# Convolution block with GRN: which blocks keep their activations on chip, where stored blocks are loaded, and the layout of the last twelve blocks

## The chip, the cores and the metric

The kernel runs on one core of one Trainium2 chip. The metric is the device time of one execution in microseconds, the median of several runs. The engines are named as in the profile: PE (matrix products), PEld (its weight loads), DVE (vector), ACT (activation functions), POOL (general purpose, here elementwise sums and the issue of some DMAs) and SP (issue of DMAs).

## The reference

The input x is an image of 512 x 512 pixels with 96 channels in bfloat16. What has to be computed, cut to its core (C = 96, E = 384 hidden channels):

```python
out = depthwise 3x3 convolution of x with dw          # zero padding
h = (out - mean_c(out)) / sqrt(var_c(out) + 1e-5)     # per pixel, over channels
h = gelu(h @ w1)                                      # [512*512, 384], tanh form
gx = sqrt(sum over all pixels of h*h + 1e-6)          # one number per hidden channel
nx = gx / (mean(gx) + 1e-6)
h = grn_gamma * (h * nx) + grn_beta + h
return x + h @ w2
```

The sum over all pixels parts the work in two. No output can be made before every pixel's hidden activations (called g here) have been made once and their squares summed. After that, the scaling by gamma * nx + 1 can be folded into the rows of w2 (the tile W2s), and beta @ w2 is a constant row (B2c), so that an output pixel is x + B2c + g @ W2s.

## The kernel before

**Blocks.** The image is cut into NBLK = 128 blocks of four rows (2,048 pixels). Phase 1 runs over slots, about one for each block and stage, and takes a block through convolution (PE), statistics over channels (squares on POOL or ACT, sums on PE), normalisation (POOL), a write of the normalised block yn to DRAM and a read back in channel layout (tile ynT), and last the first product and gelu, which gives g. g of a block is 128 partitions x 6,144 bfloat16, that is 1,536 KB; yn is 384 KB.

**g and its squares.** The gelu of a block is done in four quads of 512 pixels x 384 channels, each a PSUM area of three banks, one ACT instruction of 128x1536. A quad can be made channel-major (`cm_unit`: hidden channels on the partitions, three matmuls of 128x512) or pixel-major (`px_unit`: pixels on the partitions). The sum of squares of a channel-major quad is taken on DVE by three instructions (BATCH_NORM_STATS2, in `entry`); that of a pixel-major quad on PE, by twelve 128x128 products of g with itself that accumulate in PSUM (`gram_next` takes them from a list). `cm_quads(q)` says how many quads of block q are channel-major. The entries of DVE are collected in groups of 32; `aggregate` closes a group, and `second_moments` turns groups into sums of squares with five operations on DVE (three products and sums of two tiles, one scaling by a constant, one sum).

**What becomes of g.** g can't all stay on chip, and phase 2 needs it again. There are four kinds of blocks:
- stored (`is_whole`, 35 blocks): g is written to DRAM (`g_dram`) in phase 1 and loaded in phase 2;
- held (`HELD`, five blocks, 118, 120, 122, 124, 126): g stays in its tile until phase 2 uses it;
- recomputed (88 blocks): phase 2 reads yn back (three loads of 128 KB) and does product and gelu again, channel-major;
- of these, three blocks (`KEPT`) are recomputed from the ynT tile that is still on chip.

The tiles: `gpool` has five buffers (name g), used by phase 1 and by the held blocks. The pixel-major work of blocks 119, 121 and 123 goes to `g_over`, a view over memory that the convolution no longer needs. When the convolution's pools are closed (before the last three slots), pools for phase 2 are opened in their place: xr (five buffers), xb (three), gr (`GRB` = 3, the recomputed g, and the g of blocks 125 and 127), gld (two buffers, name gl, for stored blocks) and o (four).

**The last fourteen blocks** (from `TAIL0` = 114) have no convolution beside them; `mlp_tail` does a block as four quads one after the other. In the last twelve of all, before, a held block (four channel-major quads) alternates with one of one channel-major and three pixel-major quads, except that 116 and 117 have two of each.

**Between the phases** DVE ends the sums of squares, takes the root by Newton steps, has PE add over channels (a one-column matmul), and scales W2s. PE does up to four recompute units before that matmul and more behind it, since its order is fixed.

**Phase 2** goes through the blocks in the order of the list `ORDER`, which mixes recomputed blocks with those that need no recomputing. For position n of that list:
- five positions ahead, the load of g or yn is put into a queue (`load_rest`: stored blocks on POOL's queue, yn on SP's), and the load of x (`load_xr`, on POOL's queue);
- two positions ahead, POOL adds the constant row to x (`stage_xb`: 128x1536, result xb in float32);
- `stage_mm2` does the product with W2s, in four parts of 12 matmuls; after each DVE adds xb and writes o_sb, and `pace` puts recompute units (three matmuls and one gelu) into PE's and ACT's order, so that they are spread evenly and six ahead;
- SP stores o_sb.

PE, DVE and ACT keep the order in which the program issues instructions. POOL's and SP's instructions do so up to position 8 (`FIRST`); after that a scheduler places them by its own estimate of when they can run, which moves loads ahead or back in their queue. Helper functions record nearly all instructions, so most have the line L35 in the profile; POOL's later ones have L328 (xb), L283 (xr) and L294 (loads of stored blocks).

Of the kernel before, what the change touches and what calls it, by code (L numbers as in the profile page):

```python
# [15 lines left out]
NEWTON_ITERS = 2  # L16
FILL = (6, 15)
BATCH = 4
NHELD = 5
WHOLE = (0, 3, 7)  # L20
NTAIL = 14
GRB = 3
# [34 lines left out]
def kernel(  # L57
# [13 lines left out]
    bf16 = x.dtype  # L71
# [7 lines left out]
    NCH = E // 128  # L79
    NG = W // 128  # L80
    NBLK = H // GR
    BATCHES = batches_of(NBLK)

    QW = GR * 128
    NQ = GR * W // QW
# [2 lines left out]
    r_dram = dram.tile([NBLK, GR, W], bf16, name="r_dram")  # L88

    TAIL0 = NBLK - NTAIL  # L90
    HELD = [NBLK - 2 - 2 * i for i in range(NHELD)][::-1]
    KEPT = [NBLK - 5, NBLK - 3, NBLK - 1]

    def is_held(q):
        return q in HELD

    def is_whole(q):
        return q < TAIL0 and q % 10 in WHOLE

    def cm_quads(q):  # L100
        if is_whole(q) or is_held(q):
            return NQ
        if q > HELD[0]:
            return 1
        return 2 if q >= NBLK - 16 or (q - 1) % 10 in WHOLE else 3

    whole = [q for q in range(NBLK) if is_whole(q)]
# [17 lines left out]
    def read_spread(eng, t, q):  # L125
        rows = yn_dram[q].rearrange("(c i) (r w) -> i c r w", i=NI, r=GR)
        for i in range(NI):
            eng.dma_start(out=t[i:128:4], in_=rows[i])
# [31 lines left out]
    NYT = 6  # L160
# [3 lines left out]

    W2s = consts.tile([128, NCH, C], bf16, name="W2s")
    B2c = consts.tile([128, C], f32, name="B2c")
    free = [[q for q in range(NBLK) if is_whole(q)], list(HELD)]
    free = [v for i, q in enumerate(free[0]) for v in (free[1][i:i + 1] + [q])]
    made_q = KEPT + [q for q in range(NBLK) if not is_whole(q) and not is_held(q) and q not in KEPT]
    ORDER = []  # L170
    for i, q in enumerate(made_q):
        ORDER.append(q)
        while len(ORDER) - i - 1 < (i + 1) * len(free) // len(made_q):
            ORDER.append(free[len(ORDER) - i - 1])
    assert sorted(ORDER) == list(range(NBLK))
    nth_made = {q: n for n, q in enumerate(made_q)}
    SLOTS = [q % NYT for q in KEPT + [NBLK - 6, NBLK - 4, NBLK - 2]]

    class late:
        pass  # L180
# [1 line left out]
    gpool = ctx.enter_context(tc.tile_pool(name="g", bufs=5))  # L182
    pspool = ctx.enter_context(tc.tile_pool(name="ps", bufs=1, space=bass.MemoryType.PSUM))
    PS = pspool.tile([128, 8, W], f32, name="PS")
    p2 = ExitStack()
    SL = PXP + 2
    with ExitStack() as p1:
# [99 lines left out]
        def load_rest(n, sq, pq):  # L287
            q = ORDER[n]
            v = grp.setdefault(q, {})
            if is_held(q):  # L290
                v["g"] = gs[q]
            elif is_whole(q):
                v["g"] = late.gl.tile([128, NQ, NCH, QW], bf16, name="gl")
                pq.dma_start(out=v["g"][:].rearrange("p t j w -> p (t j w)"), in_=g_dram[whole.index(q)])  # L294
            else:
                ynt = yn_ring[SLOTS[nth_made[q] % NYT]]
                if q not in KEPT:
                    read_spread(sq, ynt, q)
                v["ynt"], v["w1"] = ynt, w1p if q in KEPT else w1s

# [220 lines left out]
        def stage_stats(b):  # L521
            k = batch_of[b]
            b0, n = BATCHES[k]
            for src, h in ((ybf[b], 0), (ysq.pop(b), 1)):
                for g in range(NG):
                    c0 = (b - b0) * NG + g
                    for i in range(NI):
                        pe.matmul(S[:, h, c0:c0 + (GR - 1) * n * NG + 1:n * NG],
                                  lhsT=src[:, i, g * 128:(g + 1) * 128], rhs=rowsel[:],
                                  start=False, stop=(i == NI - 1), skip_group_check=True)  # L530


        def stage_moments(k):
            N = BATCHES[k][1] * GR * NG
            m = small.tile([128, 2, NS], f32, name="mom")
            dve.tensor_scalar(out=m[:, :, :N], in0=S[:, :, :N], scalar1=1.0 / C, scalar2=None, op0=ALU.mult)
            dve.memset(S[:], 0.0)
            msts[k] = m
# [69 lines left out]
        def stage_turn(k):  # L608
            NT = (BATCHES[k][1] * GR * NG + 31) // 32 * 32
            rt = rtpool.tile([128, NS], bf16, name="rt")  # L610
            dve.transpose(out=rt[:, :NT], in_=rns.pop(k)[:, :NT])
            rts[k] = rt
# [59 lines left out]
        def entry(b, j, m):  # L672
            k, e = divmod(ents[b] + m, 32)
            if k not in bsts:
                bsts[k] = bstpool.tile([128, NCH, 32, 6], f32, name="bst")
            dve.bn_stats(out=bsts[k][:, j, e, :], in_=gs[b][:, m, j, :])

        def mlp_tail(b, get):
            if is_held(b) or b < HELD[0]:
                gs[b] = gpool.tile([128, NQ, NCH, QW], bf16, name="g")[:]  # L680
            elif b > NBLK - 4:
                gs[b] = late.gr.tile([128, NQ, NCH, QW], bf16, name="gr")[:]
            else:
                gs[b] = g_over
            for t in range(NQ):
                cm = t < cm_quads(b)
                (cm_unit if cm else px_unit)(gs[b], ynts[b], t)
                gram_next(1)
                if cm:
                    for j in range(NCH):  # L690
                        entry(b, j, t)
                if t == 1:
                    for k in get("turn"):
                        stage_turn(k)
                if t == 2:
                    for b2 in get("stats"):
                        stage_stats(b2)
                if t > cm_quads(b):
                    grams.extend((b, (t - 1) * QC + k * E) for k in range(0, GR, 2))
            for k in get("moments"):  # L700
                stage_moments(k)
            if cm_quads(b) < NQ:
                grams.extend((b, (NQ - 1) * QC + k * E) for k in range(0, GR, 2))
# [64 lines left out]
        def gram_next(n):  # L768
            for b, c0 in grams[:n]:
                for c1 in (c0, c0 + E):  # L770
                    for j in range(NCH):
                        v = flat(b)[:, c1 + j * 128:c1 + j * 128 + 128]
                        pe.matmul(gram[:, j, :], lhsT=v, rhs=v, start=False, stop=True, skip_group_check=True)
            del grams[:n]
# [63 lines left out]
        for s in range(last_slot + 1):  # L838
# [58 lines left out]
            else:  # L897
                b = mlp[0]
# [53 lines left out]
            if s == last_slot - 3:  # L952
                pc.close()
                late.xr = p2.enter_context(tc.tile_pool(name="xr", side="right", bufs=5))
                late.xb = p2.enter_context(tc.tile_pool(name="xb", side="right", bufs=3))
                late.gr = p2.enter_context(tc.tile_pool(name="gr", side="right", bufs=GRB))
                late.gl = p2.enter_context(tc.tile_pool(name="gld", side="right", bufs=2))
                late.o = p2.enter_context(tc.tile_pool(name="o", side="right", bufs=4))
            if s == last_slot - 2:
                for n in range(PRE):  # L960
# [5 lines left out]
            if s == last_slot:  # L966
                for n in range(PRE):
                    load_rest(n, sp, sp)
# [102 lines left out]
```

## Time and profile before

| | us |
|---|---|
| median of three runs | 1479.4 |
| the three runs | 1470.68, 1479.4, 1481.37 |
| span of the execution profiled | 1475.6 |

Of the execution profiled the page gives the span alone, from its first to its last instruction; its own time with what lies around the span is not listed beside it.

| engine | busy us | share of the span | instructions |
|---|---|---|---|
| PE | 1394.1 | 94% | 23125 |
| DVE | 1183.4 | 80% | 2174 |
| ACT | 1405.9 | 95% | 1595 |
| POOL | 1300.9 | 88% | 923 |

| stage | from us | to us |
|---|---|---|
| the last fourteen blocks' quads | about 890 | 966 |
| end of the sums, W2s | 966 | 974 |
| products of phase 2 | 974 | 1472 |

Busy time is a sum over stages with different limits; what counts is which wait ends last in a stage. A group's line names output and input tiles, shapes, count, busy time and mean duration; "idle before" is the time in which the engine waited, with the engine or DMA that ended the wait. A line of the timeline gives start and length in microseconds, the engine, its operation and how many of it are merged. Queues of DMA issue are written as POOLq and SPq.

### The profile page before, as it was taken

The numbers are of one execution on the slowest core, as the hardware profiler recorded it, in microseconds if no ns is written. First come the engines' busy times: TensorE is split into PE (matmuls) and PEld (weight loads), VectorE is DVE, ScalarE is ACT, GpSimd is POOL, SyncE is SP. The second block draws the span as 40 slices with busy tenths as digits, with TensorE's granted clock in tenths as the row PEclk, the third lists the DMA queues.
The fourth block names the chain that finished last, engine by engine and source line by source line (L and its number), as shares of the span: only waits on it lengthen the run. The fifth ranks groups of instructions, "written<-read, shape, count | busy, mean of one in ns | idle before, by whom it ended". The sixth has DMA issues, their size and how long they took to land.

```text
span 1475.6 us, 54538 instructions
## 1 busy us (share of the span) xinstructions
PE 1394.1 (94%) x23125; PEld 810.0 (55%) x23125; DVE 1183.4 (80%) x2174; ACT 1405.9 (95%) x1595; POOL 1300.9 (88%) x923
## 2 busy tenths in 40 slices
PE   8889899999899999999999998889999999999998
PEld 3434444444444444444444445457777777777776
DVE  8849989999899999999999997965555555555555
ACT  7889999999899999999998999999999999999997
POOL 3469989998899999999999998379999999999998
PEclk9999999999999999999999999999999999999999
DMA  6677778888788888888898876669999999999998
GB/s 180 197 204 231 245 231 275 249 266 240 244 254 268 262 275 239 271 258 272 249 276 247 267 230 200 177 226 366 358 328 383 402 392 392 405 381 406 389 390 315
DMA packets 167913, 422.03 MB, mean 286 GB/s; under 512 B 34326, under 2 KB 84182, under 8 KB 163190
## 3 DMA queue, kind: packets, MB, share of 16 engines
q1 hardware_dynamic: 151428, 314.98, 66.0%
q0 software_dynamic: 14880, 103.43, 18.6%
q8 instruction: 181, 2.97, 0.8%
q14 instruction: 62, 0.51, 0.1%
q10 hardware_dynamic: 1362, 0.15, 0.1%
HBM read 262.16 MB, written 156.22 MB: 284 GB/s over the span
## 4 chain that ended last, share of the span: by engine, by line
POOL 31%; PE 22%; ACT 13%; DVE 12%; DMA 11%; issue 7%; SPq 3%; POOLq 0%; ACTq 0%; DVEq 0%
PE PS L35 22%; POOL xb L328 17%; ACT g L35 8%; DVE bst L35 8%; POOL yn L35 7%; DMA xin<-in_x_dram 3%; ACT y_bf L35 3%; SPq L35 3%; DMA ynT<-yn_dram 3%; POOL xr L283 2%; DMA rbc<-r_dram 2%; DVE xT L35 2%; DMA yn_dram<-yn 2%; POOL ysq L35 1%; POOL var L35 1%
## 5 line engine op out<-in xcount | busy, mean ns | idle before, releaser
L35 ACT ACTIVATE g<-PS 128x512 bf16<-128x512 f32 (+2 forms) x1062 | 730.7, 842 | 26.0 <-PE PS L35 22.4
L35 DVE BATCH_NORM_STATS2 bst<-g 128x6 f32<-128x512 bf16 x1110 | 673.0, 672 | 23.5 <-ACT g L35 23.4
L35 ACT ACTIVATE gr<-PS 128x1536 bf16<-128x1536 f32 x360 | 498.5, 1457 | 14.8 <-PE PS L35 10.0
L35 POOL TENSOR_TENSOR yn<-y_bf,rbc 128x1536 bf16<-128x1536 bf16 x126 | 391.6, 3111 | 84.1 <-DMA rbc<-r_dram 50.5
L35 DVE TENSOR_TENSOR o_sb<-PS,xb 128x384 bf16<-128x384 f32 x512 | 277.7, 556 | 221.3 <-PE PS L35 172.0
L35 PE MATMUL PS<-xT,Wq 64*32 64x511 bf16 (+1 forms) x9198 | 347.6, 388 | 29.2 <-DVE y_bf L35 11.7
L328 POOL TENSOR_TENSOR xb<-xr,B2c 128x1536 f32<-128x1536 bf16 x118 | 368.4, 3136 | 1.5
L35 PE MATMUL PS<-ynT,w1p 128*128 128x512 bf16 x1161 | 332.7, 383 | 24.0 <-ACT g L35 5.8
L35 POOL TENSOR_TENSOR ysq<-y_bf 128x1536 bf16<-128x1536 bf16 x114 | 314.1, 2756 | 11.0 <-ACT y_bf L35 9.6
L35 PE MATMUL PS<-ynT,w1s 128*128 128x512 bf16 x1020 | 275.5, 379 | 0.0
L35 PEld LDWEIGHTS <-gr 128*128 128x128 bf16 x4296 | 212.1, 98 | 61.0 <-issue 3.0
L35 PE MATMUL PS<-W2s,gr 128*128 128x96 bf16 x4224 | 223.4, 206 | 2.0 <-DVE o_sb L35 1.8
L35 PEld LDWEIGHTS <-Wq 64*32 64x32 bf16 x9216 | 111.4, 90 | 201.4 <-issue 159.0
L35 ACT ACTIVATE y_bf<-PS 128x1536 bf16<-128x1536 f32 (+2 forms) x135 | 181.7, 1351 | 15.7 <-PE PS L35 10.6
L35 DVE STREAM_TRANSPOSE xT<-xin 128x576 f32<-128x576 f32 (+1 forms) x256 | 181.4, 748 | 12.8 <-DMA xin<-in_x_dram 10.6
L35 PEld LDWEIGHTS <-w1p 128*128 128x128 bf16 x1161 | 89.8, 98 | 180.3 <-issue 123.3
L35 PEld LDWEIGHTS <-g 128*128 128x128 bf16 (+1 forms) x1707 | 105.5, 98 | 89.1 <-issue 57.0
L35 PE MATMUL PS<-w1p,ynT 128*128 128x256 bf16 (+2 forms) x822 | 125.0, 272 | 8.0 <-ACT xT L35 3.2
L35 PE MATMUL PS<-g 128*128 128x128 bf16 x1464 | 123.1, 221 | 4.1 <-DVE PS L35 4.1
L35 PEld LDWEIGHTS <-w1s 128*128 128x128 bf16 x1020 | 81.9, 98 | 40.5
L35 PEld LDWEIGHTS <-gl 128*128 128x128 bf16 x1680 | 83.1, 98 | 30.0 <-issue 8.9
L35 PE MATMUL PS<-W2s,gl 128*128 128x96 bf16 x1680 | 90.3, 206 | 5.2 <-DVE o_sb L35 4.6
(109 smaller groups left out, 708.4 us busy)
## 6 DMA issues: line engine op xcount, KB each, us to landing
xin<-in_x_dram SPq DMA_DIRECT2D x126, 432.0 KB
g_dram<-g SPq DMA_DIRECT2D x105, 512.0 KB
gl<-g_dram POOLq DMA_DIRECT2D x35, 1536.0 KB, 10.7
yn_dram<-yn SPq DMA_DIRECT2D x512, 96.0 KB
ynT<-yn_dram SPq DMA_DIRECT2D x128, 384.0 KB
out_dram<-o_sb SPq DMA_DIRECT2D x127, 384.0 KB
xr<-in_x_dram POOLq DMA_DIRECT2D x123, 384.0 KB, 6.6
ynT<-yn_dram SPq DMA_DIRECT2D x255, 128.0 KB
```

What stands on the lines that cost most here:

```text
L35: r = f(*a, **k)
L283: pq.dma_start(out=xr[:], in_=x[0, r0:r0 + GR].rearrange("r w c -> (r w) c").rearrange("(p g) c -> p g c", g=PXP))
L328: pq.tensor_tensor(out=xb[:], in0=grp[q]["xr"][:], in1=bias[:, None, :].to_broadcast([128, PXP, C]), op=ALU.add)
```

## The change

- Seven blocks are held, not five: 116, 118, 120, 122, 124, 125 and 126. The first five lie in the five buffers of gpool; 125 and 126 lie in buffers of gr, which has five instead of three.
- Two blocks are kept as ynT (123 and 127), not three. 86 blocks are recomputed, not 88, 344 units instead of 352.
- The pool gld is gone. A stored block is loaded into a buffer of gpool, one that a held block, or an earlier stored block, has left.
- The other blocks of the last twelve (117, 119, 121, 123 and 127) have no channel-major quad: all four are pixel-major.
- `ORDER` is built anew. It begins 125 (held), 123, 127 (kept), 126 (held), 1, 2 (recomputed), 116 (held); the first stored block comes at position 13 (before: 6), and the last two are 119 and 121, recomputed (before: the last was a stored block).

```diff
-NHELD = 5
...
-    HELD = [NBLK - 2 - 2 * i for i in range(NHELD)][::-1]
-    KEPT = [NBLK - 5, NBLK - 3, NBLK - 1]
+    HELD = [NBLK - 12, NBLK - 10, NBLK - 8, NBLK - 6, NBLK - 4, NBLK - 3, NBLK - 2]
+    KEPT = [NBLK - 5, NBLK - 1]
...
         if q > HELD[0]:
-            return 1
+            return 0
...
-    free = [[q for q in range(NBLK) if is_whole(q)], list(HELD)]
-    free = [v for i, q in enumerate(free[0]) for v in (free[1][i:i + 1] + [q])]
+    stored = [q for q in range(NBLK) if is_whole(q)]
+    free = HELD[5:] + HELD[:2]
+    for i, q in enumerate(stored):
+        free.append(q)
+        free.extend(HELD[2 + i:3 + i] if i < 3 else [])
...
     for i, q in enumerate(made_q):
+        while len(ORDER) - i < 1 + (i * len(free) + 4) // len(made_q) and len(ORDER) - i < len(free):
+            ORDER.append(free[len(ORDER) - i])
         ORDER.append(q)
-        while len(ORDER) - i - 1 < (i + 1) * len(free) // len(made_q):
-            ORDER.append(free[len(ORDER) - i - 1])
+    ORDER.extend(free[len(ORDER) - len(made_q):])
...
-    SLOTS = [q % NYT for q in KEPT + [NBLK - 6, NBLK - 4, NBLK - 2]]
+    SLOTS = [q % NYT for q in KEPT + [NBLK - 6, NBLK - 4, NBLK - 3, NBLK - 2]]
...
-                v["g"] = late.gl.tile([128, NQ, NCH, QW], bf16, name="gl")
+                v["g"] = gpool.tile([128, NQ, NCH, QW], bf16, name="g")
...
-            if is_held(b) or b < HELD[0]:
+            if b < HELD[0] or b in HELD[:5]:
                 gs[b] = gpool.tile([128, NQ, NCH, QW], bf16, name="g")[:]
...
-                late.gr = p2.enter_context(tc.tile_pool(name="gr", side="right", bufs=GRB))
-                late.gl = p2.enter_context(tc.tile_pool(name="gld", side="right", bufs=2))
+                late.gr = p2.enter_context(tc.tile_pool(name="gr", side="right", bufs=GRB + 2))
```

## The prediction

> **What bounds the kernel now.** I read the chain that ended last first, then the windows by stage, the waits, and the timeline of the two places that the chain goes through. The chain by engine:
>
> ```profile
> POOL 31%; PE 22%; ACT 13%; DVE 12%; DMA 11%; issue 7%; SPq 3%; POOLq 0%; ACTq 0%; DVEq 0%
> ```
>
> POOL leads although ACT has more busy time, so the kernel has stages with different limits. The windows (columns: PE, PEld, DVE, ACT, POOL busy, clock, DMA share, GB/s) show two:
>
> ```profile
> 940.00:960.00 20.00, 15.70 (x127) 9.55 (x126) 18.11 (x38) 20.00 (x16) 4.72 (x3) 1.00 0.62 190
> ...
> 1250.00:1300.00 50.00, 49.18 (x719) 36.31 (x717) 27.55 (x51) 48.50 (x36) 48.67 (x32) 1.00 1.02 402
> ```
>
> In the end of phase 1 ACT is full, DVE near it and POOL idle. In phase 2 four resources are at 97% or more. The waits of phase 2 (who waited for whom: us, times, longest) and POOL's timeline (start, length) tell them apart:
>
> ```profile
> DVE o_sb L35 <- POOL xb L328: 46.0, 54, 2.1
> POOL xr L283 <- POOL xb L328: 14.8, 50, 0.3
> ...
> POOL xb L35 <- DVE o_sb L35: 10.7, 3, 9.9
> ```
> ```profile
> 1181.51 6.22 POOL L328 TENSOR_TENSOR xb<-xr,B2c 128x1536 f32<-128x1536 bf16 x2
> 1187.66 1.11 POOL L283 DMA_DIRECT2D xr<-in_x_dram  x2
> 1188.79 3.14 POOL L328 TENSOR_TENSOR xb<-xr,B2c 128x1536 f32<-128x1536 bf16 x1
> 1192.22 0.56 POOL L283 DMA_DIRECT2D xr<-in_x_dram  x1 [0.30 <-POOL xb L328]
> 1192.78 0.53 POOL L294 DMA_DIRECT2D gl<-g_dram  x1
> 1193.33 6.21 POOL L328 TENSOR_TENSOR xb<-xr,B2c 128x1536 f32<-128x1536 bf16 x2
> ```
>
> POOL waits only for itself: 50 gaps of 0.30 us, where an xr load needs the buffer of the sum just ahead of it. Its one long wait (9.9) is before 979.64, and the other two add 0.75 us. The adds on DVE wait 54 times for POOL. So from 979.64 to the end of the last xb at 1469.91 POOL runs without a hole: 490.3 us = 125 xb x 3.09 + 121 xr x 0.556 + 34 gl x 0.536 + 50 x 0.30 + 0.75, some 3 us of seams left. Three blocks cost it 11.82 us (1181.51 to 1193.33), 3.94 each. ACT needs 88 x 4 / 128 = 2.75 gelus a block; in its fullest stretch 27 took 37.51 us, 1.389 each, so 3.82. PE: 12 product matmuls every 0.51 us, 0.65 more for a recompute unit, so 4 x 0.51 + 2.75 x 0.65 = 3.83. Both are 3% behind POOL.
>
> What starts that POOL chain is the end of the statistics:
>
> ```profile
> 945.96 7.22 DVE L35 BATCH_NORM_STATS2 bst<-g 128x6 f32<-128x512 bf16 x12 [1.75 <-ACT g L35]
> 953.10 1.86 DVE L35 BATCH_NORM_STATS2 bst<-gr 128x6 f32<-128x512 bf16 x3
> 954.88 0.40 DVE L35 BATCH_NORM_STATS2 mom<-bst 128x6 f32<-128x36 f32 x3
> 955.20 0.27 DVE L35 TENSOR_REDUCE tot<-bst 128x3 f32<-128x108 f32 x1
> 955.40 0.24 DVE L35 TENSOR_TENSOR parts<-mom 128x72 f32<-128x72 f32 x1
> ...
> 965.96 2.02 DVE L35 TENSOR_TENSOR parts<-mom 128x6 f32<-128x6 f32 x1
> ```
> ```profile
> 958.68 9.27 POOL L35 TENSOR_TENSOR xb<-xr,B2bc_f 128x1536 f32<-128x1536 bf16 x3 [15.28 <-DMA xr<-in_x_dram]
> ```
>
> A block with all four quads channel-major costs DVE 7.22 us, while ACT makes a block every 5.37 (blocks 124 and 125 start at 944.21 and 949.58). And a product of 128x6 took 2.02 us, whose like takes 0.17; it ended at 967.98, when POOL's three sums ended (967.95).
>
> **The change part by part.**
>
> *Two blocks fewer are recomputed*: 8 gelus (8 x 1.389 = 11.1 us of ACT), 24 matmuls (8 x 0.65 = 5.2 us of PE), three ynT loads fewer (one block is read back less). Every block still has its xr load, its xb and its adds. I cost this at nothing: POOL's chain covers it.
>
> *Quads*. In the last twelve blocks 28 are channel-major instead of 29, 20 pixel-major instead of 19. ACT has 48 as before. The one more quad gives PE 12 gram matmuls (0.5 us per six), in a stretch where PE is busy 15.7 of 20: nothing. After the last gelu the same 12 remain (966.14 to 966.98).
>
> *Where the quads lie* is what costs. Before, held and one-quad blocks alternate to the end, 7.22 + 1.86 against 10.7 us of ACT. Now 124, 125 and 126 are channel-major in a row, 36 statistics, then 127 without any. DVE's order as built is: 24 statistics (124, 125), the closing of a group, the second moments of all groups but the last, 12 statistics (126), the last group. With ACT's times unchanged, 124's first again starts at 945.96; 24 x 7.22 / 12 end at 960.40; the group's closing (954.88 to 955.40) takes 0.52, so the second moments start at 960.92. Before they ran at 955.40 to 956.71 (1.31), POOL idle. Now POOL's three sums (958.68, 961.77, 964.86, to 967.95) lie across them: the xr loads that these wait for hang on SP's last read of yn, not on DVE or ACT, so they don't move. Of the five operations four have two SBUF inputs. What one costs beside a running sum is shown by the 2.02 row only: it waited until the sum's end. From below, DVE waits once (0.85, to 961.77) and then does all five before POOL starts again. From above it is out until 967.95, or one operation passes at each seam; both end near 969.0, 6.8 later than the 962.2 without a collision. I take the upper end: the next sum is queued with its data there, and DVE's operations depend on each other, leaving a gap after each.
>
> The Trainium skill ("SBUF — State Buffer", section "Who interferes with whom") says that a VectorE instruction with two SBUF inputs and a GpSimd instruction that reads SBUF exclude each other, that the first to start holds the port for its whole length, and that the loser is fully blocked. By that rule the collision costs the upper end, since POOL takes the port back in every gap; by the row read alone it could be 0.85. The 2.02 us row agrees with it.
>
> So 126's statistics end at 969.0 + 7.22 = 976.2, the last group takes 0.33, its products 0.17 (POOL is done by then) and 1.06 (967.98 to 969.04): the sum starts at 977.8 instead of 969.04, **+8.8 us**. All behind it (root, W2s at 973.96, the first block's product, the fourth xb at 979.64) keeps its distances. Queued behind this wait on PE is the one-column matmul, with the recompute units past the fourth behind it: ACT idles some 9 us. On POOL, xb 4 waits for the first block's adds.
>
> *Order of blocks*. The first product block is held (125), not recomputed; the queue of units ahead of it is the same six. With less to recompute among the first blocks the two waits of POOL for DVE (0.75) go. In the order as built 44 xr loads stand just behind the sum that they need, not 50: -1.8. One stored block's load comes after the fourth xb that came before it: +0.54. Together **-2.0**.
>
> *Loads of stored blocks into the held tiles*. Five tiles circulate, not two; in POOL's queue the loads stand up to 13 blocks ahead of use, not 4, but each still two sums behind the block whose tile it takes, as before, where all 33 took 533 to 551 ns. So no wait; if PE fell behind by a block, each could wait up to a block's 3.9 us, and all xb's behind it.
>
> Sum: +8.8 - 2.0 = **+6.8**. The execution profiled has a span of 1475.6 us; what lies around it is not listed. The median of the three runs is 3.8 above (0.26%), and they spread over 10.7 us. Added to the median: **1486 us**.
>
> **The rivals.**
>
> *A, the forecast*, 1486: chance 0.50.
>
> *B, the gate slips little*: DVE gets its five operations through at the first seam, or the sums start later than 962. Slip 2.0 (no collision: 971.0) to 2.9, less 2.0: 0 to +0.9, 1480. For it: nobody has been seen at a seam. Against: gaps between DVE's operations. 0.20.
>
> *C, not slower: ACT sets phase 2's pace*. Then the 11.1 us count: 8.8 - 11.1 = -2.3, or 2.0 - 11.1 = -9.1: 1470 to 1477. It decides where ACT's time per block (3.82) exceeds POOL's (3.94), and there are the last 35 us, where the chain is PE's. Against: POOL without a hole. 0.15.
>
> *D, slower by over 1%: DMA becomes the bound*. Its share is 1.0 already. Groups of two recomputed and one stored block now follow each other almost without the longer groups between. One moves 3 x 768 + 2 x 384 + 1536 KB = 4.72 MB; at 11.8 us that is 400 GB/s. If DMA can hold only 380, a group takes 12.4, 0.6 more for some 26 groups: +16 above A, 1502; at 394 it is +5, 1491. Above 1494 from 388 down. Against: such groups already ran at 11.82, xr landing stays at 6.5 to 6.8 us in every 60 us window from 1120 on, and single slices show 449. 0.15.
>
> **How the numbers follow.** A measurement of this kernel, with runs 0.7% apart, can tell about 1% from no change, 1464.6 to 1494.2. A and B lie inside, C with them but for its far end and a low run; D is half outside. Faster 0.05, same 0.82, slower 0.13. Range 1472 to 1494: A and B with the medians' scatter, the near part of C, the lower part of D.
>
> **What would show it.** In the changed profile: 36 statistics in a row broken by products of some 3 us each or one of 7 us, ending at 967.9 to 969; W2s at about 982.7; ACT idle about 9 us before it; the fourth xb near 988; from there POOL without a hole for about 488 us, with 44 gaps of 0.30; more DVE time waiting for xb than 46 us; ACT's share down. It is wrong if POOL waits for DVE or PE in phase 2, if xr landing rises above 8 us, if W2s is ready by 977, or if the fourth xb to the last takes under 480 us.

## The result, and the profile after

| | before | after |
|---|---|---|
| median, six runs each on one chip | 1477.35 us | 1488.47 us |
| the runs | 1470.68 to 1481.37 | 1486.73 to 1493.49 |
| span of the execution profiled | 1475.6 | 1488.1 (own time 1489.92) |
| mean granted clock | 0.995 | 0.989 |

The ratio is 1.0079, interval [1.0056, 1.0103]: the median is 11.1 us longer, where the prediction had 6.8 us more, 1486. The span of the executions profiled grew by 12.5 us. The stretch from the last blocks' statistics to the fourth xb, where POOL's chain of phase 2 starts, is called the gate below. Line numbers moved: helpers are L34 now, POOL's sums L331, xr loads L286, loads of stored blocks L297.

The place that the prediction turned on, in the timeline of DVE (start, length, operation, idle time before and its releaser):

```profile
946.91 7.22 DVE L34 BATCH_NORM_STATS2 bst<-g 128x6 f32<-128x512 bf16 x12 [3.53 <-ACT g L34]
954.04 7.20 DVE L34 BATCH_NORM_STATS2 bst<-gr 128x6 f32<-128x512 bf16 x12
...
961.68 1.90 DVE L34 TENSOR_TENSOR parts<-mom 128x72 f32<-128x72 f32 x1
963.62 6.17 DVE L34 TENSOR_TENSOR parts<-parts,mom 128x72 f32<-128x72 f32 x2
969.82 0.21 DVE L34 TENSOR_SCALAR parts<-parts 128x72 f32<-128x72 f32 x1
970.19 7.21 DVE L34 BATCH_NORM_STATS2 bst<-gr 128x6 f32<-128x512 bf16 x12
...
978.87 0.23 DVE L34 TENSOR_REDUCE sums<-parts 128x3 f32<-128x78 f32 x1 [0.24 <-DVE parts L34]
...
983.43 0.56 DVE L34 TENSOR_SCALAR W2s<-w_sb,sc 128x96 bf16<-128x96 bf16 x3
```

and of POOL beside it:

```profile
960.35 9.33 POOL L34 TENSOR_TENSOR xb<-xr,B2bc_f 128x1536 f32<-128x1536 bf16 x3 [15.17 <-ACT gr L34]
...
991.45 3.12 POOL L34 TENSOR_TENSOR xb<-xr,B2c 128x1536 f32<-128x1536 bf16 x1 [20.55 <-DVE o_sb L34]
```

POOL's three sums run from 960.35 to 969.68. The first product of DVE takes 1.90 us, the second product and the sum behind it 6.17 (all three have two inputs), and the next operation, with one input, starts at 969.82. So one operation of DVE came through for each sum of POOL, as in the upper end of the forecast, and 126's statistics had to wait behind them, until 970.19. From the first statistic of block 124 to the sum of squares (`sums`, 978.87) it is 31.96 us, where before it was 23.08 (945.96 to 969.04): 8.9 more.

What follows that was not foreseen stands in the windows of 2 us (length, then busy us of PE, PEld, DVE, ACT, POOL, then PE's clock, the share of DMA and GB/s):

```profile
972.00:974.00 2.00, 0.26 (x2) 0.00 (x0) 2.00 (x5) 2.00 (x2) 0.00 (x0) 1.00 0.75 307
974.00:976.00 2.00, 0.00 (x0) 0.00 (x0) 2.00 (x4) 0.09 (x1) 0.00 (x0) 0.65 0.00 0
976.00:978.00 2.00, 0.00 (x0) 0.00 (x0) 1.97 (x9) 0.00 (x0) 0.00 (x0) 0.50 0.00 0
...
986.00:988.00 2.00, 2.00 (x15) 1.17 (x13) 0.56 (x1) 1.27 (x2) 0.00 (x0) 0.50 0.00 0
988.00:990.00 2.00, 2.00 (x25) 1.39 (x23) 0.91 (x2) 1.91 (x2) 0.00 (x0) 0.94 0.00 0
```

PE waited 9.9 us for DVE, its clock went to 0.50, and it was still there while PE did the first product. From W2s (end 983.99) to the fourth xb (991.45) it took 7.46 us; before 5.68 (973.96 to 979.64).

From there POOL carries the end, as before. Who waited for whom after 980 (us, times, longest):

```profile
DVE o_sb L34 <- POOL xb L331: 56.1, 54, 3.3
...
POOL xb L34 <- DVE o_sb L34: 20.9, 2, 20.6
...
POOL xr L286 <- POOL xb L331: 13.1, 44, 0.3
...
POOL xr L286 <- issue: 2.4, 1, 2.4
```

The gaps of 0.30 are 44 instead of 50, and POOL's waits for DVE are 20.6 (the one ahead of 991.45) and 0.3. New is one hole of 2.4 us that no wait explains. From 991.45 to the last xb's end (1481.94) it is 490.5 us, before 490.3.

The 12.5 us of the span are made up so: 0.95 at the end of phase 1 (946.91 against 945.96), 8.9 from the first statistic to the sum of squares, 0.2 from there to W2s, 1.8 from W2s to the fourth xb at half clock, 0.2 in POOL's chain, 0.5 behind its end.

### The profile page after: what moved, and what is told of

The parts are those of the page before. It is cut to its first block, busy times and chain, and to the rows that moved or that the text cites. A ratio compares the mean times of both kernels' runs of the same rounds, so it can differ in the third digit from the quotient of the medians.

```text
span 1488.1 us, 54515 instructions
## 1 busy us (share of the span) xinstructions
PE 1391.7 (94%) x23116; PEld 809.8 (54%) x23116; DVE 1185.6 (80%) x2171; ACT 1397.5 (94%) x1587; POOL 1299.2 (87%) x923
## 4 chain that ended last, share of the span: by engine, by line
POOL 26%; PE 25%; DVE 17%; DMA 13%; ACT 8%; issue 6%; SPq 4%; POOLq 0%; ACTq 0%; DVEq 0%
PE PS L34 25%; POOL xb L331 12%; DVE bst L34 11%; POOL yn L34 8%; ACT g L34 5%; DMA ynT<-yn_dram 5%; SPq L34 4%; DVE xT L34 3%; DMA yn_dram<-yn 3%; DMA rbc<-r_dram 3%; ACT y_bf L34 3%; POOL ysq L34 2%; POOL xr L286 1%; POOL nt L34 1%; DMA xin<-in_x_dram 1%
## 5 line engine op out<-in xcount | busy, mean ns | idle before, releaser
L34 ACT ACTIVATE g<-PS 128x512 bf16<-128x512 f32 (+2 forms) x1054 | 718.4, 834 | 22.7 <-PE PS L34 18.8
L34 DVE BATCH_NORM_STATS2 bst<-g 128x6 f32<-128x512 bf16 x1098 | 665.7, 672 | 27.2 <-ACT g L34 27.0
L34 ACT ACTIVATE gr<-PS 128x1536 bf16<-128x1536 f32 x356 | 495.6, 1455 | 33.8 <-PE PS L34 28.5
L34 POOL TENSOR_TENSOR yn<-y_bf,rbc 128x1536 bf16<-128x1536 bf16 x126 | 391.3, 3108 | 86.6 <-DMA rbc<-r_dram 38.6
L34 DVE TENSOR_TENSOR o_sb<-PS,xb 128x384 bf16<-128x384 f32 x512 | 276.4, 556 | 224.9 <-PE PS L34 164.9
L34 PE MATMUL PS<-xT,Wq 64*32 64x511 bf16 (+1 forms) x9198 | 346.2, 389 | 26.7 <-DVE y_bf L34 8.0
L331 POOL TENSOR_TENSOR xb<-xr,B2c 128x1536 f32<-128x1536 bf16 x118 | 367.9, 3132 | 1.3
L34 PE MATMUL PS<-ynT,w1p 128*128 128x512 bf16 x1146 | 330.5, 385 | 26.6 <-ACT g L34 4.8
L34 POOL TENSOR_TENSOR ysq<-y_bf 128x1536 bf16<-128x1536 bf16 x114 | 313.7, 2752 | 11.1 <-ACT y_bf L34 9.5
L34 PE MATMUL PS<-ynT,w1s 128*128 128x512 bf16 x1008 | 273.1, 380 | 1.6 <-DMA ynT<-yn_dram 1.6
L34 PEld LDWEIGHTS <-g 128*128 128x128 bf16 (+1 forms) x3339 | 185.1, 98 | 116.9 <-issue 65.7
L34 PEld LDWEIGHTS <-gr 128*128 128x128 bf16 x4272 | 210.8, 98 | 61.8 <-issue 6.9
L34 PE MATMUL PS<-W2s,gr 128*128 128x96 bf16 x4224 | 222.8, 207 | 4.5 <-DVE o_sb L34 4.2
L34 PEld LDWEIGHTS <-Wq 64*32 64x32 bf16 x9216 | 111.3, 90 | 197.8 <-issue 155.8
L34 ACT ACTIVATE y_bf<-PS 128x1536 bf16<-128x1536 f32 (+2 forms) x135 | 181.8, 1352 | 19.2 <-PE PS L34 12.8
L34 DVE STREAM_TRANSPOSE xT<-xin 128x576 f32<-128x576 f32 (+1 forms) x256 | 181.6, 749 | 10.2 <-DMA xin<-in_x_dram 9.6
L34 PEld LDWEIGHTS <-w1p 128*128 128x128 bf16 x1146 | 88.5, 98 | 183.8 <-issue 122.2
L34 PE MATMUL PS<-w1p,ynT 128*128 128x256 bf16 (+2 forms) x828 | 125.8, 272 | 8.1 <-DMA ynT<-yn_dram 2.1
L34 PE MATMUL PS<-g 128*128 128x128 bf16 x1416 | 118.7, 220 | 3.9 <-DVE PS L34 3.7
L34 PE MATMUL PS<-W2s,g 128*128 128x96 bf16 x1920 | 103.3, 207 | 5.2 <-DVE o_sb L34 5.2
L34 PEld LDWEIGHTS <-w1s 128*128 128x128 bf16 x1008 | 80.3, 98 | 41.7 <-issue 2.1
L34 PEld LDWEIGHTS <-ynT 128*128 128x128 bf16 x828 | 64.6, 97 | 31.0 <-issue 10.9
```

Source lines behind the costliest of these rows:

```text
L34: r = f(*a, **k)
L331: pq.tensor_tensor(out=xb[:], in0=grp[q]["xr"][:], in1=bias[:, None, :].to_broadcast([128, PXP, C]), op=ALU.add)
```

## The experiments

Each is compared with the kernel before, run on the same chip; the chips differ, so times of two rows are compared by way of the kernel before. The column us is the median. The ratio is not the quotient of the two medians, from which it differs by up to 0.3%.

| run | made from | edit | us | before, us | ratio, interval |
|---|---|---|---|---|---|
| a_late | after | second moments in one go, at the end | 1479.24 | 1474.53 | 1.0037 [1.0016, 1.0058] |
| a_fill | after | 40 unused matmuls in the gate | 1488.56 | 1474.53 | 1.0077 [1.005, 1.0104] |
| b_px | before | 119, 121, 123, 125 and 127 pixel-major | 1470.58 | 1472.26 | 0.9986 [0.9962, 1.0009] |
| b_xrsp | before | xr loads on SP's queue | 1505.17 | 1474.53 | 1.0209 [1.0178, 1.0239] |
| a_late_xrsp | after | a_late's edit and b_xrsp's | 1513.79 | 1474.53 | 1.0234 [1.0203, 1.0264] |
| b_pair | before | x of two blocks in one load | 1505.58 | 1472.26 | 1.0202 [1.0145, 1.0259] |
| a_late_pair | after | a_late's edit and b_pair's | 1512.57 | 1472.26 | 1.0272 [1.0203, 1.034] |
| b_skip | before | every fourth xb left out | 1522.71 | 1478.14 | 1.0313 [1.0278, 1.0349] |
| a_late_skip | after | a_late's edit and b_skip's | 1507.49 | 1478.14 | 1.019 [1.0142, 1.0238] |
| b_inorder | before | POOL in program order | 1474.91 | 1475.83 | 0.998 [0.9953, 1.0006] |
| a_late_inorder | after | a_late's edit and b_inorder's | 1490.12 | 1475.83 | 1.0088 [1.0053, 1.0123] |
| b_inorder_half | before | program order, half of x's bytes | 1467.31 | 1476.7 | 0.9941 [0.9924, 0.9959] |

### The collision: a_late

The theory is the forecast's: DVE's second moments meet POOL's sums and are shut out. The rival is that the row of 36 statistics itself is what costs (126's twelve come last).

```diff
             if s == last_slot - 2:
-                second_moments(0, NACC - 1)
...
-        second_moments(NACC - 1, NACC)
+        second_moments(0, NACC)
```

> The changed kernel with the second moments of all groups taken once, after the last group, instead of before 126's statistics; nothing is left out. Theory A (the gate, by the port collision): 126's statistics follow 125's at once, about 961.7 to 968.9 us in the changed kernel's profile; five operations then find POOL's three sums ended or in their last 0.7 us; the sum over groups starts at about 971.4 instead of 978.9, PE idles 2.5 us instead of 9.9, so its clock does not fall and W2s to the fourth xb takes 5.7 us again, not 7.5. In all 7.5 + 1.8 = 9.3 us less than the changed kernel: 1479, 0.1% above the kernel before. Rival Q (36 statistics in a row are the cost, not the collision): the sum over groups stays near 977, the time within 2 us of 1488.

Measured: 1479.24, 4.7 us above the kernel before on its chip, so of the 11.1 us 4.7 stayed. DVE's timeline, with nothing between the 36 statistics, and POOL's:

```profile
957.15 7.21 DVE L34 BATCH_NORM_STATS2 bst<-gr 128x6 f32<-128x512 bf16 x12
...
964.60 0.26 DVE L34 TENSOR_TENSOR parts<-mom 128x78 f32<-128x78 f32 x1
964.90 0.56 DVE L34 TENSOR_TENSOR parts<-parts,mom 128x78 f32<-128x78 f32 x2
```
```profile
952.72 9.27 POOL L34 TENSOR_TENSOR xb<-xr,B2bc_f 128x1536 f32<-128x1536 bf16 x3 [14.73 <-PE PS L34]
```

POOL's sums are over at 961.99, and the same three operations take 0.26 and 0.56 us, not 1.90 and 6.17. From the first statistic (942.38) to the sum of squares (966.13) it is 23.75 us, from there to the fourth xb (976.69) 10.56; before 23.08 and 10.60. With the collision nearly all of the 8.9 us is gone, and the rival falls. Only operations with two inputs were shut out: the statistics of DVE, which have one, ran beside the same sums of POOL at their usual 7.2 us for twelve, in the kernel before beside those that began at 958.68:

```profile
956.71 7.22 DVE L35 BATCH_NORM_STATS2 bst<-g 128x6 f32<-128x512 bf16 x12
```

The row of 36 statistics is not free, though. The 8.9 us are the sum of three parts. The second moments, from their first product to the next statistic, take 8.51 us (961.68 to 970.19) instead of 1.31 (955.40 to 956.71), which is 7.2 more. Six statistics more lie between the two ends (36 against 30), 3.6 us. And the last group's first product, which waited for POOL before (2.02 us), no longer does (0.17), 1.85 less. In a_late the 7.2 are gone, and so is the separate pass of 1.31, so that 0.7 is left.

How much the collision costs depends on when POOL's sums begin. a_fill (next section) has the collision too, but in its profile they began 10.9 us behind the first statistic of 124 (942.97) and not 13.4, so that DVE met the second of them and waited for two:

```profile
953.91 9.31 POOL L34 TENSOR_TENSOR xb<-xr,B2bc_f 128x1536 f32<-128x1536 bf16 x3 [14.81 <-DMA xr<-in_x_dram]
```
```profile
957.74 2.49 DVE L34 TENSOR_TENSOR parts<-mom 128x72 f32<-128x72 f32 x1
960.26 3.37 DVE L34 TENSOR_TENSOR parts<-parts,mom 128x72 f32<-128x72 f32 x2
```

From the first statistic to the sum of squares (972.71) it was 29.74 us there, 6.7 more than before and not 8.9.

That a_late still lies 0.37% above the kernel before is not the gate's doing: in the execution profiled 0.7 us of it at most. Its phase 2, from the fourth xb to the end of the span, is 498.1 us there, before 496.0; it has the 2.4 us hole, and PE waits 6.7 us for loads of yn, which it did not before. No run takes these two away, so what costs the other 4 us is not shown.

### The clock: a_fill

The idle time of PE is filled with matmuls into a PSUM bank that nobody reads; the collision stays.

```diff
+        for k in range(40):
+            pe.matmul(PS[:, 6, :], lhsT=zrow[:, :128], rhs=zrow[:], start=True, stop=True)
         pe.matmul(tot_ps, lhsT=ones_f[:], rhs=rs_[:], start=True, stop=True)
```

> The changed kernel with 40 matmuls of zeros (128x512 each, to a free PSUM bank) ahead of the one-column matmul that PE waits for, 8.5 us of work where PE idles 9.9. Nothing is left out; the extra matmuls compute nothing that is used. Theory: the granted clock of 0.50 between 978 and 986 comes from PE's idling, and it makes the first block's product slow: with the fill the clock stays at 1.0, W2s to the fourth xb takes 5.7 us, not 7.5, the time falls by 1.8 us to 1486.7. Rival: the first block is slow for another reason (ACT restarting, banks): the distance stays 7.5 us and the time 1488.5 or more.

The windows of this kernel around the same wait:

```profile
974.00:976.00 2.00, 2.00 (x11) 0.94 (x10) 1.62 (x11) 0.00 (x0) 0.00 (x0) 1.00 0.00 0
...
978.00:980.00 2.00, 1.68 (x19) 1.08 (x18) 0.99 (x5) 2.00 (x2) 0.00 (x0) 1.00 0.00 0
```

The clock stays at 1.00, and from W2s (end 978.32) to the fourth xb (983.96) it is 5.64 us, about the 5.68 of the kernel before. So it is the idling that halves the clock, and 1.8 us is its price at that place. The median, 1488.56, shows nothing of it: the expected gain is smaller than the interval, the filling itself held the one-column matmul up by 0.5, and POOL's chain was 493.1 in the execution profiled. That filling saves time is not shown.

### The layout alone: b_px

In the kernel before, the last five blocks that are not held (119, 121, 123, 125 and 127) have four pixel-major quads; everything else stays, the second moments and the two channel-major quads of 116 and 117 too.

```diff
         if q > HELD[0]:
-            return 1
+            return 0
```

> The kernel before with one part of the change alone: the blocks of the last twelve that are not held (119, 121, 123, 125, 127) have four pixel-major quads instead of three and one channel-major. Theory A: held blocks still alternate with others, so DVE is never behind; the second moments run before POOL's three sums start, the last group still meets the third of them: W2s as before, the time within 3 us of the kernel before. Rival (the layout itself costs, by grams on PE that make ACT wait in the last blocks): ACT waits of 1 us and more for PE in the last twelve blocks, as the changed kernel shows at 928 and 935, and 2 to 5 us more.

0.9986 [0.9962, 1.0009]: no cost of the pixel-major quads can be told, and ACT does not wait for PE in the last twelve blocks. The second moments ran from 944.77 to 946.08, ahead of POOL's sums, and took 1.31 us as before. One product still meets the last of POOL's three sums, which began at 949.03 and ended at 958.31:

```profile
955.39 2.95 DVE L35 TENSOR_TENSOR parts<-mom 128x6 f32<-128x6 f32 x1
958.37 0.37 DVE L35 TENSOR_TENSOR parts<-parts,mom 128x6 f32<-128x6 f32 x2
```

It lasted until that sum's end; the next two, with POOL done, took 0.37 together.

### Is POOL what sets phase 2's pace?

The prediction costed eight gelus fewer at nothing, since POOL had no hole in 490 us. The gain did stay away (a_late has hardly any gate cost left and is not faster than before), but that does not show that POOL is the reason. If POOL is the reason, then less work for POOL must give time, until ACT and PE (3.82 and 3.83 us a block against 3.94) are the next bound: 128 blocks by 0.11, about 14 us. The rival is DMA, at a share of 1.0.

**xr loads on SP's queue** (b_xrsp, a_late_xrsp) take 0.56 us per block and the gaps from POOL.

```diff
-                load_xr(n + PRE, pq)
+                load_xr(n + PRE, sq)
```

> The kernel before with every load of x in phase 2 issued by SP instead of POOL, so that POOL has 3.09 + 0.15 us a block instead of 3.94. Theory A (POOL sets the pace of phase 2): the pace goes to ACT and PE at 3.82 to 3.83 a block, 0.11 x 125 = 14 us less, 1463 to 1466; POOL is below 88% busy and waits for DVE. Rival C (ACT sets it already) or D (DMA does): the time stays within 3 us of 1477. Rival S: SP's queue, where stores wait for DVE ahead of loads, becomes late, and the time grows.

> The changed kernel with both edits: second moments taken late, and loads of x issued by SP. Theory A: with POOL relieved, the 11.1 us of ACT that the change saves are worth something: ACT 2.69 x 1.389 = 3.73 us a block, PE 3.79; the time is that of the kernel before with loads by SP less 5 (PE) to 9 us (ACT, 11.1 less 2 of gate): 1455 to 1461. Rival (ACT's units were not what the change saves, or DMA is the next bound): no better than the kernel before with loads by SP.

Both became slower by 2%. A window and some waits of b_xrsp:

```profile
1200.00:1250.00 50.00, 45.84 (x671) 33.82 (x669) 26.54 (x49) 45.18 (x34) 40.00 (x17) 1.00 1.00 374
```
```profile
DVE o_sb L35 <- DMA out_dram<-o_sb: 57.6, 25, 3.7
...
POOL xb L328 <- DMA xr<-in_x_dram: 32.1, 14, 3.6
```
```profile
SPq L356 <- DMA xr<-in_x_dram: 61.6, 29, 5.5
```

POOL has time (40 of 50 us busy), and PE does 671 matmuls instead of 714 in that window of the kernel before. DMA is at its share of 1.00 with only 374 GB/s, loads and stores are late. But SP's one queue now holds three kinds of transfers in one order, and in it the stores (L356) waited 61.6 us for loads of x, the last line says. That is rival S of the expectation. So the edit brought a cost of its own: the run relieves POOL and gains nothing, but does not tell POOL, bytes and queue apart.

**x of two blocks in one load** (b_pair, a_late_pair) leaves the loads on POOL. Its double buffers take the room of one o buffer.

```diff
+            if n % 2:
+                return
+            q0, q1 = sorted(ORDER[n:n + 2])
+            xr = late.xr.tile([128, 2, PXP, C], bf16, name="xr")
...
-    name="xr", side="right", bufs=5
+    name="xr", side="right", bufs=3
-    name="o", side="right", bufs=4
+    name="o", side="right", bufs=3
```

> The kernel before with the x of two blocks loaded by one DMA, still in POOL's queue (three double buffers for xr instead of five single ones, three for o instead of four, for space). POOL issues 61 loads instead of 123: at 0.556 each and with most of the 0.30 gaps gone, 34 to 45 us less of its 490. Theory A (POOL sets the pace of phase 2): the pace passes to PE and ACT, 3.83 a block instead of 3.94, 0.11 x 125 = 14 us less: 1461. Rival C (PE and ACT set it already): within 3 us of the kernel before. Rival D (DMA is as near a bound): the stretches with a stored block in every three stay at about 11.8 us for three blocks, the gain is under 5 us and xr landing rises.

> The changed kernel with second moments taken late and with x loaded for two blocks at once. Theory A: once POOL no longer covers them, the eight gelus and 24 matmuls that the change saves count: PE 3.79, ACT 3.73 a block, 0.15 x 125 = 19 us less than the changed kernel with late moments (1479): 1460, and 1 to 6 us less than the kernel before with double loads in what its profile shows between the fourth xb and the end. Rival D: DMA at 400 GB/s holds both at the same time, since the bytes differ by 0.2% only.

Again 2% and more slower. A load of two took POOL 0.74 us, where two took 1.11. The waits of b_pair point to a cause:

```profile
DVE o_sb L35 <- DMA out_dram<-o_sb: 39.9, 28, 4.6
POOL xb L331 <- DVE o_sb L35: 32.5, 33, 5.3
```

Before, the adds waited for a store 2.1 us in all. As far as the waits tell, it is the o buffer given up that shows, so this run is no test of POOL.

**Every fourth xb left out** (b_skip, a_late_skip). These kernels leave x out of the output of 30 blocks.

```diff
+            if ORDER.index(q) >= 8 and ORDER.index(q) % 4 == 3:
+                grp[q]["xb"] = None
+                return
...
-                                   in1=xb[:, sub * GPS:(sub + 1) * GPS, :], op=ALU.add)
+                                   in1=B2c[:, None, :].to_broadcast([128, GPS, C]) if xb is None
+                                   else xb[:, sub * GPS:(sub + 1) * GPS, :], op=ALU.add)
```

> The kernel before, in which POOL leaves out its sum xb for every fourth block of phase 2 from the eighth on (30 of 128); DVE adds the constant row B2c alone for these, so x is missing from their output. Their x is still loaded, so DMA moves the same bytes; buffers and queues are the same. POOL has 93 us less. Theory A (POOL sets phase 2's pace at 3.94 us a block): the pace passes to PE and ACT at 3.83, the fourth xb to the end shrinks by about 14 us, time about 1459. Rival C (PE and ACT set it): within 3 us of the kernel before. Rival D (DMA is a bound as near): in the stretches with one stored block in three the pace stays at 11.8 us for three blocks, the gain is under 5 us.

> The changed kernel with second moments taken late, and the same 30 sums of POOL left out. If A holds: PE 3.79 and ACT 3.73 a block, about 19 us less than the changed kernel with late moments, and 5 us less between the fourth xb and the end than the kernel before with the sums left out: the recompute units that the change saves are worth something once POOL no longer covers them. If D holds (400 GB/s, bytes the same but for 0.2%): no less than the kernel before with the sums left out, and more where stored blocks come one in three.

They failed as a test too. With nobody to read them, the scheduler put each next xr load right behind the unread one, and POOL stood there until that had landed:

```profile
POOL xr L283 <- DMA xr<-in_x_dram: 127.8, 28, 7.3
```
```profile
1150.00:1200.00 50.00, 50.00 (x738) 37.25 (x736) 29.00 (x53) 49.59 (x37) 34.09 (x24) 1.00 1.01 392
```

But in the stretch of the second line PE ran without a pause, 738 matmuls in 50 us where the kernel before had 719, although POOL stood still twice in it (2.6 and 5.5 us): with POOL relieved, PE can be the bound.

**POOL in program order** (b_inorder, a_late_inorder). No instruction is taken away. The loads only stand where the program puts them, not right behind the sum whose buffer they take, so the gaps of 0.30 go (50 x 0.30 = 15 us).

```diff
-            sq, pq = (sp, pool) if n < FIRST else (nc.sync, nc.gpsimd)
+            sq, pq = sp if n < FIRST else nc.sync, pool
```

> The kernel before with POOL's instructions of phase 2 kept in the program's order to the end (before, only up to position 8), so that no load of xr stands right behind the sum whose buffer it needs; nothing is left out, buffers and sums are the same. None of the 50 gaps of 0.30 us is left in the order as built. Theory A (POOL sets phase 2's pace): 15 us less of POOL's 490 from the fourth xb to the last, until PE and ACT hold it at 3.83 a block: 1462 to 1468. Rival C or D (PE and ACT, or DMA, set it): the same 490, within 3 us of the kernel before, and POOL's gaps come back as waits for DVE, PE or a load.

> The changed kernel with second moments taken late, and POOL's order of phase 2 kept as in the program: no gap of 0.30, loads of stored blocks five positions ahead instead of 13. Theory A: 13 us less than the changed kernel with late moments for the 43 gaps, and PE's and ACT's lower load (3.79, 3.73) lets POOL run free: 1463 to 1466, not above the kernel before with the same order; POOL waits less for DVE and PE than there. Rival: the pace was DMA's, nothing changes from 1479.

b_inorder: 0.998 [0.9953, 1.0006], so a gain of at most 7 us. Its windows:

```profile
1100.00:1150.00 50.00, 50.00 (x737) 37.20 (x735) 28.44 (x52) 49.58 (x37) 49.62 (x31) 1.00 1.02 401
1150.00:1200.00 50.00, 50.00 (x737) 37.20 (x734) 28.45 (x52) 49.53 (x37) 49.52 (x31) 1.00 1.01 402
1200.00:1250.00 50.00, 48.13 (x711) 35.80 (x709) 27.27 (x50) 47.67 (x36) 47.50 (x30) 1.00 1.00 389
```

The chain that ended last is PE's in this kernel:

```profile
PE 42%; ACT 16%; DMA 12%; POOL 12%; DVE 10%; issue 4%; SPq 3%; ACTq 0%; POOLq 0%; DVEq 0%
```

So POOL is relieved here. Up to 1200 PE is full. From there it has pauses again, though POOL's gaps are gone: from 1200 on DVE waits 9.4 us for stores, and POOL 6.3 for DVE and 4.5 ahead of loads of stored blocks. DMA is at its share of 1.0 with about 400 GB/s. The execution profiled was the slowest of twelve (1481.3 us, the median 1474.91), so it may show more pauses than most. a_late_inorder, which neither theory had expected to be slower than a_late, is 14.3 us above the kernel before on its chip, a_late 4.7 on its own. There PE waits for the loads of yn, and why these come late was not tested:

```profile
PE PS L34 <- DMA ynT<-yn_dram: 22.0, 19, 2.6
DVE o_sb L34 <- DMA out_dram<-o_sb: 14.9, 11, 3.2
```

**Program order, and half of x's bytes** (b_inorder_half). What ate the gain of b_inorder: the bytes, or the order of queues and buffers? This is the same kernel with some 13% less to move in phase 2, and the same work on POOL. It leaves half of x out: eight of a partition's sixteen pixels get the x of the other eight.

```diff
-            pq.dma_start(out=xr[:], in_=x[0, r0:r0 + GR].rearrange(...))
+            pq.dma_start(out=xr[:, :PXP // 2], in_=x[0, r0:r0 + GR].rearrange(...)[:, :PXP // 2])
...
-            pq.tensor_tensor(out=xb[:], in0=grp[q]["xr"][:], ...)
+            pq.tensor_tensor(out=xb[:].rearrange("p (k g) c -> p k g c", k=2),
+                             in0=grp[q]["xr"][:, None, :PXP // 2, :].to_broadcast([128, 2, PXP // 2, C]), ...)
```

> The kernel before with POOL kept in program order (no xr load right behind the sum whose buffer it takes, so none of the 50 gaps of 0.30), and of each block's x only the first eight of a partition's sixteen pixels are loaded (192 KB instead of 384); POOL's sum reads them twice, so that its work is the same and the last eight output pixels of a partition have the x of the first eight. DMA has 128 x 192 KB = 25 MB less to move in phase 2, of some 402 GB/s x 490 us = 197 MB, 13%. The program order alone left POOL without gaps, had PE full from 1000 to 1200 (737 matmuls per 50 us, 719 before), and lost it again later; median 0.998 of the kernel before. Theory L, the bytes ate it (DMA's share was 1.02 at about 400 GB/s): now the gain is kept to the end, PE is at 730 or more matmuls per 50 us in all windows from 1000 to 1400, the last 270 us gain 2.5% too, the time is 490 x 0.025 = 12 us below the kernel before, 1463 to 1467, ratio 0.990 to 0.993, with DMA's share below 0.95. Theory O, the order of the queues or of the buffers ate it, not the bytes: the waits of 1200 and later stay (POOL for DVE 20, gl 4.5, out 11), ratio 0.996 to 1.000. Theory P, POOL's own work is the pace after all (its chain was 488 us there, as long as before): then also 0.996 to 1.000, but POOL's sums follow each other without a wait for DVE or DMA.

1467.31, ratio 0.9941 [0.9924, 0.9959], 9.4 us below the kernel before, a little less than the 12 of theory L. PE's windows stay full to the end:

```profile
1100.00:1150.00 50.00, 50.00 (x737) 37.22 (x735) 28.82 (x53) 49.58 (x37) 49.48 (x32) 1.00 0.97 358
...
1300.00:1350.00 50.00, 50.00 (x733) 37.19 (x732) 28.44 (x53) 49.51 (x37) 49.64 (x31) 1.00 0.97 357
```

Most of the waits from 1200 on are gone (for stores 2.0 us instead of 9.4, POOL for DVE 1.0 instead of 6.3, ahead of loads of stored blocks none instead of 4.5), and the chain that ended last, by engine, is PE's still more:

```profile
PE 49%; ACT 14%; DMA 10%; DVE 10%; POOL 9%; issue 4%; SPq 3%; POOLq 0%; ACTq 0%; DVEq 0%
```

From the fourth xb (978.25) to the end of the span (1464.6) it is 486.4 us, where the kernel before has 496.0, and b_inorder too (983.51 to 1479.5), though in its slowest execution. The ratios, 0.9941 and 0.998, are 0.4% apart, and their intervals just overlap. So fewer bytes kept a gain that the order of POOL alone did not show. That x itself came earlier is not the reason: POOL waited for it only 0.3 us in b_inorder. What fits is that phase 2 has two bounds of about the same height, POOL's queue and DMA, and that lifting the first alone shows the second. This is argued from two runs. Whether fewer bytes alone, with the gaps left in POOL's queue, would gain was not tried. And DMA's share is a weak sign: theory L expected it below 0.95, and from 1100 on it was still 0.96 to 0.97 with the waits gone.

No version that does the whole computation was faster than the kernel before beyond what can be told.

## Why the prediction was right, and where it was not

**The collision, +8.8**: right in place and mechanism, and a_late takes it away by moving DVE's operations out of the sums' way. Its parts, 2.0 without a collision and 6.8 for it, measured 1.7 and 7.2. That the sum came out within 0.1 us (8.9) is partly luck, since the same code slipped by 6.7 in a_fill's execution. The upper end was the right end: the first three operations with two SBUF inputs each waited for the end of one sum of POOL. The rule of the Trainium skill that the prediction weighed ("SBUF — State Buffer", section "Who interferes with whom") is borne out by 1.90 and 6.17 us against 0.26 and 0.56. Rival B, that DVE comes through at the first seam, falls. That POOL's three sums "don't move" was inexact: they started 1.7 us later, DVE's operations 0.8, and the overlap stayed; in a_fill they started 2.5 us earlier, counted from 124's first statistic.

**"All behind it keeps its distances"** is the step that failed. The prediction named the one-column matmul that PE waits with and ACT's idle 9 us, and did not ask what idling does to PE: its clock fell to 0.50, which cost 0.2 us up to W2s and 1.8 to the fourth xb.

**The order of blocks, -2.0**: the 44 gaps came as forecast, and POOL's waits for DVE in phase 2 went down to 0.3 us. A hole of 2.4 us took it back, and the chain was 0.2 longer instead of 2.0 shorter. This term was mis-sized by 2.2 for a reason that stays open (below).

**Fewer recomputed units at nothing**: right in its result. Rival C (ACT sets the pace, down to 1470) falls: a_late, with all but 0.7 us of the gate's cost gone, is at 1479, not below the kernel before. The reason given was at most half of it. POOL's chain is one bound, but b_inorder, which relieves it, gains 7 us at most, and b_inorder_half, with fewer bytes as well, 9.4. So DMA is probably another, and the 14 us between POOL and ACT and PE were not to be had by relieving POOL alone.

**Rival D**, DMA as the bound of the changed kernel: not as the kernel stands, since POOL's chain kept its length. It stood closer than its chance said: when POOL was relieved in the changed kernel (a_late_inorder), PE waited 22.0 us for yn, and the gain was negative.

**Loads into held tiles without a wait**: right; the g loads took 533 to 536 ns each on POOL, and waited 0.4 us in all. **Quads at nothing**: right as far as b_px can tell.

The remaining 0.95 at the end of phase 1 and 0.5 behind POOL's chain are within what executions differ by (a_late's profile has the same first statistic at 942.38, 4.5 us earlier).

**The time itself**: in the profiles the change was 12.5 us, 5.7 more than forecast, namely 2.0 by the clock, 2.2 by the order of blocks and 1.5 by the rest just named. That 1486 came so near to 1488.47 is luck in part: the prediction added its 6.8 us to the median of three runs, 1479.4, and six runs have 1477.35, so the base was 2.05 too high.

## What to carry to other kernels

Where operations with two SBUF inputs on DVE can meet a row of POOL's sums, count up to one whole sum for each of them, and move them behind POOL's work rather than ahead of DVE's next work; here two lines shortened the gate by 10.2 us in the profiles (44.5 to 34.3) and the distance to the kernel before from 11.1 to 4.7 us. A long wait of PE can have a second price in its clock: here 2.0 us after 9.9 of waiting. An engine without a hole is a bound, but not always the only one: before its relief is priced, look at which waits come up when it is relieved, and test by relieving both at once. A DMA share near 1.0 does not settle it: it was 1.00 at 374 GB/s in b_xrsp and 0.97 at 357 in b_inorder_half, where hardly anything waited for DMA.

## What the runs showed that was not expected

- PE's clock. After PE's last matmul (about 972.3) the window from 974 to 976 has 0.65, and then 0.50 until about 988, some 6 us after PE went on at 982.15. In a_late PE was never idle that long there, and the clock stayed at 1.00. The Trainium skill ("TensorE: Matmul & The Clock Gate", section "Part 1: The HAM clock gate (the "warmup" mystery)") says that an idle array falls to half rate after about 3.4 us and comes back after as long a time of sustained work. Here the fall came sooner, some 2.3 us after the last matmul (windows of 0.4 us have 1.00 up to 974.4 and 0.50 from 974.8 on), and the return took longer, some 6 us, with a PE that was not quite full at first (1.85 of 2 us in the window from 982).
- A hole without a wait. In POOL's timeline of the changed kernel:

```profile
1324.46 0.57 POOL L286 DMA_DIRECT2D xr<-in_x_dram  x1
1327.39 0.55 POOL L286 DMA_DIRECT2D xr<-in_x_dram  x1 [2.36 <-issue]
```

  It is there in a_late (2.38) and a_fill (2.37) as well, 336 to 337 us behind the fourth xb each time, at the same load in the order of POOL's instructions, so it hangs on a place in the program. The kernel before has none, but b_pair (1.90) and b_skip (2.88), which are made from it, do. What it is stays open.
- The same x loads from SP's queue let DMA move 374 GB/s in a window at a share of 1.00, from POOL's queue 396 (the kernel before, 1200 to 1250). Whether that is the queue or the order of the transfers in it was not told apart.
